# Bank sets, scalings, taps and an order of additions: one rescheduling of a fused convolution and channel MLP

## The chip, the cores and the metric

One core of a Trainium2 chip. The metric is the device time of one execution in microseconds (us), median over several runs. Ratios are the mean time of one kernel's fast runs over that of the other's of the same rounds, so not quite the ratio of the medians quoted beside them.

Engine names as the profile has them: PE is TensorE, PEld its weight loads, DVE is VectorE, ACT is ScalarE, POOL is GpSimd.

## The reference, cut to what matters

```python
def _attn_ref(x, weight):                  # x: 8 x 4224 x 192, weight: 8 heads x 7 taps
    w = softmax(weight)                    # over the taps
    # causal convolution of 7 taps along the sequence, one weight per head of 24 channels
    return np.einsum('hk,bskhg->bshg', w, x_unf)

def _moe_ref(x, g_ln, w_ch1, w_ch2):       # x: the result of the above
    xn = (x - mean) / sqrt(var + 1e-6) * g_ln
    return x + np.maximum(xn @ w_ch1, 0.0) @ w_ch2      # 192 -> 768 -> 192
```

## The kernel before

The rows are cut into 18 groups. For each group g the "up" product (w1, Relu) and the "down" product (w2) run on PE; beside them DVE does five of the seven convolution taps for group g+1, ACT the first two taps for group g+2 (the second through a buffer `tb` and an accumulating DMA, y<-tb), and the output of g-1 is scaled by the row's 1/sigma on ACT and added to the output by DMA. The down product is done in seven products of half size instead of eight (from sums of quarters, on DVE). In "mixed" groups (6, 8, ... 16) most of the up product is done so as well; two chunks of it stay plain. The sums of y that this takes lie in the room of `tb`.

Names in the code below: in the up product a11 to a22 are the quarters of y, b11 to b22 those of w1, s1 to s4 sums of quarters of y, c11 to c22 the quarters of the result; the down product has the same with the hidden values and w2. `w1sums` and `w2sums` are sums of quarters of the weights. The banks of `chain` add up several products in turn; those of `other` take one product each. To evict is to copy a set of banks out of PSUM, which ACT does here (1.87 to 1.88 us for a set of 128x2048, means of L596 and L510 in the kernel before). A matmul of the code stands as two records in the profile: 24 of them are x48 there.

The kernel takes eight banks of PSUM, in turn in two sets of four:

```python
    def take_set():
        i = (turn[0] + 3) // 4 * 4 % 8
        turn[0] = i + 4
        return all_banks[:, i : i + 4]
```

The up product of a mixed group, cut:

```python
        banks = plain(PAIR)                       # takes a set, 24 matmuls of 512 columns
        scale(g - 1, 0, 4)
        evict_up(g, PAIR, whole, banks)
        conv(g + 1, 2, 6)                         # DVE
        chain, other = take_set(), take_set()
        rows_of_tiles(chain, a11, b11, True, False)
        evict(chain, c11)
        ...                                       # a12 x b21, s2, s3, s1: in turn in other and chain
        rows_of_tiles(other, a22, w1sums[:, 3], False)
        evict(other, late[0])                     # the parts buffer
        scale(g - 1, 7, 8)
        add_to_out(g - 1, 0, 8)
        ...
        rows_of_tiles(chain, s4, b22, False)
        evict(chain, c12, True)
        nc.scalar.activation(c11, c11, AF.Relu)
        lower_sum(g, (PAIR,)); lower_sum(g, range(PAIR))   # DVE, cut to one line
        conv(g + 1, 6, K)
        banks = plain(PAIR + FC)                  # the next set in turn: the chain's
        evict_up(g, PAIR + FC, whole, banks)
        nc.scalar.activation(c22, c22, AF.Relu)
```

The down product, cut (`some_taps(n)` issues n of the 16 instructions of the first two taps for g+2; `product` ends in three copies on ACT unless told otherwise):

```python
        product(0, a[:, 0, 0], b[0], c11, True)
        if g in MIXED:
            scale(g - 1, 8, m); add_to_out(g - 1, 8, m)
            some_taps(1)
        else:
            some_taps(3)
        product(1, a[:, 1, 0], w2sums[:, 2], c22, True);        some_taps(3)
        product(1, a[:, 1, 1], w2sums[:, 3], parts[0], False);  some_taps(3)
        product(1, a[:, 0, 1], b[2], None, True);               some_taps(3)
        ...                                       # half sums on DVE
        product(0, a[:, 1, 1], w2sums[:, 1], c21, False);       some_taps(2)
        product(0, a[:, 0, 0], w2sums[:, 0], parts[1], False);  some_taps(2)
        product(0, a[:, 0, 1], b[3], c12, False);               some_taps(len(todo))
```

## Time and profile before

| | before |
|---|---|
| time, median of the first 3 runs (later of 4) | 1022.95 us (1022.73) |
| span of the profiled run | 1022.5 us |
| PE busy | 992.4 us, 97% |
| DVE busy | 884.6 us, 87% |
| PE idle in the body, 276.6 to 953.4 us | 676.80 - 658.49 = 18.3 us |

The last row is from the windows of the kernel before, from the first mixed group's start to the end of the last one. Columns: stretch, its length, then for PE, PEld, DVE, ACT and POOL the busy time with the number of instructions, then the granted clock, the DMA share and GB/s.

```profile
276.60:953.40 676.80, 658.49 (x11024) 461.53 (x11020) 598.75 (x990) 410.89 (x852) 54.20 (x64) 0.99 0.52 127
```

A clock of 0.99 as a mean over 677 us hides four short stretches at one half, called half-clock windows below. The ScalarE timeline of group 12 at the start of the down product (columns: start, duration, engine, line, operation, tiles, shapes, number; in brackets the idle time before and what ended it):

```profile
684.37 3.23 ACT L812 ACTIVATE ot<-ot,r 128x192 f32<-128x192 f32 x9
687.49 0.62 ACT L367 ACTIVATE y<-xg,taps 128x384 f32<-128x384 f32 x1
688.00 0.91 ACT L728 COPY cs<-ps 128x256 f32<-128x256 f32 x3
```

Nine scalings and one tap stand ahead of the copies of c22, which PE's third down product waits for.

### The profile page before, as it was taken

The numbers are of one execution on the slowest core, as the hardware profiler recorded it, in microseconds if no ns is written. First come the engines' busy times: TensorE is split into PE (matmuls) and PEld (weight loads), VectorE is DVE, ScalarE is ACT, GpSimd is POOL, SyncE is SP. The second block draws the span as 40 slices with busy tenths as digits, with TensorE's granted clock in tenths as the row PEclk, the third lists the DMA queues.
The fourth block names the chain that finished last, engine by engine and source line by source line (L and its number), as shares of the span: only waits on it lengthen the run. The fifth ranks groups of instructions, "written<-read, shape, count | busy, mean of one in ns | idle before, by whom it ended". The sixth has DMA issues, their size and how long they took to land. (4 is left out here: it accounts for less than half of the span.)

```text
span 1022.5 us, 37346 instructions
## 1 busy us (share of the span) xinstructions
PE 992.4 (97%) x16914; PEld 710.1 (69%) x16914; DVE 884.6 (87%) x1622; ACT 586.9 (57%) x1243; POOL 81.5 (8%) x110
## 2 busy tenths in 40 slices
PE   7999999999989999999999999989999999989997
PEld 6888674578575875758666686756857578575776
DVE  7999998899889797998979979799796989979707
ACT  6547464546576564665657665675656746574451
POOL 2001101000010000101001100110001000010000
PEclk9999999999999999999999999999999999999999
DMA  6343818535366364654636645466355663263031
GB/s 190 116 179 52 213 20 235 180 63 145 111 123 199 70 158 120 115 191 85 190 67 115 195 91 179 98 141 172 62 174 109 133 194 64 86 127 68 3 64 68
DMA packets 18702, 126.88 MB, mean 124 GB/s; under 512 B 2415, under 2 KB 3183, under 8 KB 13678
## 3 DMA queue, kind: packets, MB, share of 16 engines
q0 software_dynamic: 12096, 66.75, 33.3%
q1 hardware_dynamic: 6142, 57.73, 14.9%
q8 instruction: 132, 2.16, 0.8%
q14 instruction: 28, 0.23, 0.1%
q10 hardware_dynamic: 304, 0.00, 0.0%
HBM read 38.95 MB, written 50.23 MB: 87 GB/s over the span
## 5 line engine op out<-in xcount | busy, mean ns | idle before, releaser
L520 PE MATMUL ps<-yt,w 32*128 32x256 f32 (+6 forms) x6624 | 435.2, 417 | 14.0 <-ACT ht L596 12.6
L520 PEld LDWEIGHTS ps<-yt,w 32*128 32x128 f32 x6624 | 337.2, 186 | 109.1 <-issue 56.4
L394 DVE SCALAR_TENSOR_TENSOR y<-xg,taps,y 128x408 f32<-128x408 f32 (+5 forms) x734 | 365.9, 577 | 30.0 <-DMA y<-tb 23.9
L722 PE MATMUL ps<-ht,w2sums 128*32 128x256 f32 (+2 forms) x4320 | 238.7, 378 | 3.3 <-ACT cs L728 2.7
L687 DVE TENSOR_TENSOR ht<-ht 128x1088 f32<-128x1088 f32 (+2 forms) x162 | 184.4, 1208 | 35.6 <-ACT part L728 24.5
L722 PEld LDWEIGHTS ps<-ht,w2sums 128*32 128x32 f32 x4320 | 139.3, 110 | 97.3 <-ACT cs L728 5.5
L722 PE MATMUL ps<-ht,w 128*32 128x256 f32 (+2 forms) x3240 | 182.0, 378 | 0.0
L722 PEld LDWEIGHTS ps<-ht,w 128*32 128x32 f32 x3240 | 103.8, 110 | 73.9 <-issue 8.3
L508 ACT ACTIVATE ht<-ps 128x256 f32<-128x256 f32 (+2 forms) x312 | 100.8, 410 | 92.6 <-PE ps L520 86.4
L728 ACT COPY cs<-ps 128x256 f32<-128x256 f32 (+2 forms) x180 | 64.0, 371 | 119.2 <-PE ps L722 119.2
L510 ACT ACTIVATE ht<-ps 128x2048 f32<-128x2048 f32 (+5 forms) x48 | 63.3, 1318 | 97.7 <-PE ps L520 97.7
L812 ACT ACTIVATE ot<-ot,r 128x192 f32<-128x192 f32 x247 | 93.8, 459 | 4.9 <-DVE ot L787 4.9
L367 ACT ACTIVATE y<-xg,taps 128x408 f32<-128x408 f32 (+5 forms) x137 | 71.7, 591 | 5.8 <-DVE st L421 5.3
L421 DVE BATCH_NORM_STATS2 st<-y 128x6 f32<-128x192 f32 x264 | 70.1, 341 | 0.0
L787 DVE STREAM_TRANSPOSE ot<-cs 128x512 f32<-128x512 f32 (+2 forms) x90 | 57.7, 684 | 5.9 <-ACT cs L728 3.3
L380 ACT ACTIVATE tb<-xg,taps 128x384 f32<-128x384 f32 (+1 forms) x112 | 62.6, 618 | 0.0
L405 DVE STREAM_TRANSPOSE yt<-y 128x3072 f32<-128x3072 f32 (+5 forms) x19 | 56.2, 2957 | 4.2 <-PE ps L520 2.4
L816 POOL DMA_DIRECT2D out_dram<-ot x34 | 29.6, 884 | 364.4 <-ACT ot L812 186.2
L669 PE MATMUL ps<-ht,w 128*32 128x192 f32 (+3 forms) x1152 | 51.5, 339 | 0.0
L383 POOL DMA_DIRECT2D y<-tb x28 | 24.9, 1051 | 330.6 <-ACT cs L728 188.4
L520 PE MATMUL ps<-ysums,w1sums 32*128 32x256 f32 x864 | 48.1, 376 | 2.4 <-DVE ysums L571 2.4
L520 PEld LDWEIGHTS ps<-ysums,w1sums 32*128 32x128 f32 x864 | 45.5, 185 | 4.5 <-issue 3.5
(104 smaller groups left out, 496.6 us busy)
## 6 DMA issues: line engine op xcount, KB each, us to landing
y<-tb POOLq DMA_DIRECT2D x21, 768.0 KB, 6.0
out_dram<-ot POOLq DMA_DIRECT2D x20, 768.0 KB, 6.8
xg<-in_x_dram SPq DMA_DIRECT2D x6, 2208.0 KB, 15.8
xg<-in_x_dram SPq DMA_DIRECT2D x6, 2112.0 KB, 12.1
out_dram<-y SPq DMA_DIRECT2D x6, 1632.0 KB, 6.6
out_dram<-y SPq DMA_DIRECT2D x6, 1536.0 KB, 6.1
ht<-parts POOLq DMA_DIRECT2D x6, 1024.0 KB, 7.4
y<-tb POOLq DMA_DIRECT2D x7, 864.0 KB, 10.0
```

The lines of the kernel that those rows point to most:

```text
L367: nc.scalar.mul(dst, src, tap)
L380: nc.scalar.mul(tb[g][:, 0:n, cs], xg[g][:, 1 : 1 + n, cs], taps[:, h, 1:2])
L394: nc.vector.scalar_tensor_tensor(out=y[g][:, 0:n, cs], in0=t[:, k : k + n, cs], scalar=taps[:, h, k : k + 1], in1=y[g][:, 0:n, cs], op0=AL ...
L421: nc.vector.bn_stats(out=sums[g][:, j, :], in_=y[g][:, j, :])
L508: nc.scalar.activation(dst[:, q], src[:, q], AF.Relu)
L510: nc.scalar.activation(dst, src, AF.Relu)
L520: nc.tensor.matmul(banks[:, q, i * w : i * w + w], right[rows, c, P * i : P * i + P], left[rows, :, c, :], start=(first and c == 0 and i = ...
L687: nc.vector.tensor_tensor(a[:, *dst, f], a[:, *left, f], a[:, *right, f], op=op)
L722: nc.tensor.matmul(dst[C * q : C * q + C, 0:w], right[:, f, C * c : C * c + C], left[:, f, q], start=(first and f == 0), stop=(f == FC - 1 ...
L728: nc.scalar.copy(to[:, c], dst[:, 0:w].rearrange("p (j t) -> p j t", t=t))
L787: nc.vector.transpose(ot[:, 0:n, C * c : C * c + C], flat[:, c].rearrange("p (j t) -> p j t", t=C))
L812: nc.scalar.mul(ots[g][:, j, :], ots[g][:, j, :], rstd[g][:, j : j + 1])
```

## The change

Its intent: (1) the last plain chunk goes into the other bank set, so that PE need not wait for the eviction of the chain just before it; (2) the scalings are spread so that they fall where ACT has time; (3) the first two taps are issued sooner in odd groups, so that the room of `tb` is free when DVE wants it, and in mixed groups they are spread so that they end one product sooner; (4) in groups 3 and 4 the partial sums are added ahead of the statistics.

```diff
@@ up product of a mixed group
 (cut: plain(f) no longer takes a set itself; it is given its banks)
-        banks = plain(PAIR)
-        scale(g - 1, 0, 4)
-        evict_up(g, PAIR, whole, banks)
+        other, chain = take_set(), take_set()
+        turn[0] += 4
+        plain(PAIR, other)
+        scale(g - 1, 0, 7)
+        evict_up(g, PAIR, whole, other)
         conv(g + 1, 2, 6)
-        chain, other = take_set(), take_set()
 (cut: the four single scalings are now 7..11 in place of 4..8)
         conv(g + 1, 6, K)
-        banks = plain(PAIR + FC)
-        evict_up(g, PAIR + FC, whole, banks)
+        scale(g - 1, 11, 14)
+        plain(PAIR + FC, other)
+        evict_up(g, PAIR + FC, whole, other)
@@ down product
+        taps_behind = [3, 3, 3, 3, 2, 2]
+        if g in MIXED:
+            taps_behind = [0, 3, 3, 4, 3, 3]
+        elif g + 1 in MIXED:
+            taps_behind = [4, 4, 4, 4, 0, 0]
 (cut: some_taps(n) becomes some_taps(taps_behind[i]) behind products 1 to 6)
-            scale(g - 1, 8, m)
+            scale(g - 1, 14, m)
@@ end of a group
+        for half in range(last, 2):
+            finish_fast(g, half, *parts)
         if not last and not mixed and g + 1 not in MIXED:
             moments(g + 1)
             if g % 2 == 0:
                 root(g)
-        for half in range(last, 2):
-            finish_fast(g, half, *parts)
```

## The prediction

> **What bounds the kernel now.** I read the page first (part 1, part 2, part 5), then the waits, then the timelines of one pair of groups, 580 to 725 us, and last the windows around the waits.
>
> Part 1 and part 5 of the page:
>
> ```profile
> PE 992.4 (97%) x16914; PEld 710.1 (69%) x16914; DVE 884.6 (87%) x1622; ACT 586.9 (57%) x1243; POOL 81.5 (8%) x110
> ...
> L520 PE MATMUL ps<-yt,w 32*128 32x256 f32 (+6 forms) x6624 | 435.2, 417 | 14.0 <-ACT ht L596 12.6
> ```
>
> PE is the bound: 992.4 of 1022.5 us, so only 30.1 us are idle. The waits of PE name nearly all of it:
>
> ```profile
> PE ps L520 <- ACT ht L596: 12.6, 6, 2.7
> PE ps L344 <- POOL room L272: 4.9, 1, 4.9
> PE ps L722 <- ACT cs L728: 2.7, 5, 0.6
> PE ps L520 <- DVE ysums L571: 2.4, 3, 0.8
> PE ps L520 <- ACT ht L508: 1.4, 1, 1.4
> PE ps L722 <- DVE ht L687: 0.5, 1, 0.5
> ```
>
> (columns: us in total, times, longest). Six waits on L596 are one for each mixed group (6, 8, ... 16): the last plain chunk is put in the banks of the chain, and must wait until ScalarE has emptied them into c12. PE's timeline in group 12 and ScalarE's in group 14:
>
> ```profile
> 667.41 2.77 PE L520 MATMUL ps<-ysums,w 32*128 32x256 f32 x48
> 672.83 7.11 PE L520 MATMUL ps<-yt,w 32*128 32x512 f32 x48 [2.66 <-ACT ht L596]
> ```
> ```profile
> 792.37 1.87 ACT L596 COPY parts<-ps 128x2048 f32<-128x2048 f32 x1 [0.70 <-PE ps L520]
> 794.13 0.46 ACT L812 ACTIVATE ot<-ot,r 128x192 f32<-128x192 f32 x1
> 794.91 1.88 ACT L596 ACTIVATE ht<-ps 128x2048 f32<-128x2048 f32 x1 [0.33 <-PE ps L520]
> ```
>
> The wait costs more than it lasts. The same 24 matmuls of 512 columns take 7.11 to 7.13 us in groups 6, 8, 10, 12 and 5.43 us in 14 and 16. The windows tell why (the third number from the end, ahead of DMA share and GB/s, is the granted clock):
>
> ```profile
> 673.00:675.50 2.50, 2.50 (x12) 1.05 (x16) 2.50 (x6) 1.57 (x1) 0.00 (x0) 0.50 1.04 152
> 797.00:802.00 5.00, 5.00 (x48) 2.21 (x48) 5.00 (x9) 1.59 (x1) 0.00 (x0) 1.00 1.03 177
> ```
>
> After the wait in four of six groups the clock falls to one half for a while; 7.12 - 5.43 = 1.7 us each, hidden in "busy".
>
> DVE (87%) is the nearest rival. It waits in every odd group for the transfer y<-tb to release the buffer that the sums of y take:
>
> ```profile
> DVE ysums L570 <- DMA y<-tb: 44.4, 6, 8.0
> DVE y L394 <- DMA y<-tb: 23.9, 5, 5.4
> ```
>
> [...] half clock, for 2 x 1.7 = 3.4 us. [...] a 2.0 us wait does not always cost a window: 4 of 6 here, the others (14, 16) with the same wait did not. [...] nine scalings in a row take 3.23 us, 0.36 each. [...] y<-tb, the adds of partial products and the adds to the output share one software queue; the page has all of them there (33.3% of 16 engines).
>
> **The change, part by part** (T is the end of s4 x b22, 670.2 in group 12, which nothing ahead of it moves).
>
> (1) Other bank set. The last plain chunk now needs the eviction of a22's product into the parts buffer, not that of c12. In group 14: begun 792.37, 1.87 long, done 794.24; s4 ends at 792.06 + 2.80 = 794.86. So 0.6 us to spare. Only group 12 is late: its eviction began at 668.79 after 1.80 us for the transfer ht<-parts, and ends at 670.66, 0.5 us after T. The wait shrinks from 12.6 to some 0.5 us: about 12 us off the path. The sets of all products keep their relation (the counter is moved on by one set, so the down product starts one set further): its first two columns take the chain's banks, free at T + 1.9; its third takes the plain chunk's, evicted by T + 5.43 + 2.0 = T + 7.4, needed at T + 5.43 + 2.7 = T + 8.1. That was so before.
>
> (2) The half clock. With no wait there is nothing left to throttle: 4 x 1.7 = 6.8 us in the profiled run. The plain runs differ by 1.85 us (1022.51 to 1024.36), about one window, so I take 3 to 4 windows, 5.1 to 6.8.
>
> (3) Scalings. The same 17 a group: 7 before the first plain eviction (7 x 0.36 = 2.6 us, from 648.0 to 650.6; the eviction can start at 652.1), 4 single ones as before, 3 in the shadow of the last plain chunk (ScalarE there: c12 1.9, Relu of c11 1.9, scalings 1.1, done at T + 4.9, chunk at T + 5.4), 3 instead of 9 in the down product. It is these 9 (684.37, 3.23 us) that delay the copies of c22, for which PE waits 0.56 us five times: 2.7 us gone.
>
> (4) Taps of odd groups. Before, the last two of 16 wait behind product 6 and end at 644.1; now four follow each of the first four products. ScalarE in group 11: parts copied by 630.7, then eight at 0.55 = 635.1. The transfer is issued 9 us sooner; it took 10.2 us from issue (644.4 to 654.7), so it lands near 645.5, before DVE asks at 647.9. DVE's 44.4 us of waiting fall to near 0, the sums are there before PE wants them: 2.4 us of PE. In mixed groups the taps end behind product 6 rather than 7: some 3 us sooner, DVE's 23.9 us roughly halve, off the path.
>
> (5) Partial sums ahead of the statistics: reaches groups 3 and 4 only, as the condition excludes all others. In group 4 ScalarE waited 6.2 us for DVE (the addition at L785 frees the hidden tile); the addition moves from 217.6 to about 210, and PE's 1.4 us goes. DVE loses about 1 us there, with 2.4 us of slack at its transpose.
>
> **Does DVE allow it?** PE comes to the down product 2.0 + 1.7 us sooner in each mixed group, and its fifth product needs DVE's half sums. DVE in group 12 needs 36.8 us from the first sum of y (654.67) to the first half sum (691.43). Started at 647.9, with some 1.3 us of waiting for the Relu of c11, it is there at 686.1. The half sum can begin near the end of the third product, T + 17.1 = 687.3. Margin 1.2 us, and as much again while the fourth product runs (4.07 us against 3.4 us of half sums). In group 16 PE already waited 0.5 us for DVE; that goes too.
>
> **Sum.** 12.1 + 2.7 + 2.4 + 1.4 + 0.5 = 19.1 us of waits, and 5.1 to 6.8 us of clock: 24 to 26 us. From 1022.95: 997 to 999. I add about 0.7 us for small waits: 998.5, 2.4% faster.
>
> **The rivals.** (A) DVE takes over as bound in the mixed groups: if y<-tb lands late because the load of x (issued 622.5, 12.1 us to landing) and the store of y share the engines then, the start slips. Against it: the load is nearly over at 635; the slack is about 2 to 3 us. Were it 3 us over, 6 x 3 = 18 us return at most; likelier 1 us in each, 6 us: 1004. (B) The clock stays throttled, or only the waits count: had the half clock another cause than the wait, 6.8 us stay: 1005. Against it, the two groups right after equal waits run at 5.43 us, and no stretch without a wait is throttled. (C) ScalarE or the software queue becomes the new wait at the same place: the add to the output of the first 8 rows is now issued some 3 us sooner (its scalings are done), in a stretch where the windows show DMA at 1.0 of its share, and may hold up the adds to c22, needed by a Relu at T + 7.4. They landed at about 673.6; slack 4 us, and 4 more before PE needs it. That leaves at most 1 us in each group. (D) The waits were hidden anyway: speaks against it that PE is the bound in the whole body and the chain that ended last ends with 33.55 us of L520 and 20.61 of L722 on PE.
>
> **Range and chances.** The floor is 1022.95 - 19.6 - 6.8 = 996.5. Rivals A to C each give back 0 to 6 us. Range 995.5 to 1004. Faster by over 2% means below 1002.5: 0.84; within 2%: 0.15; slower: 0.01.
>
> **What would show it.** Right: no wait of PE on the c12 eviction, at most 1 us on L596's others; the last plain chunk at 5.4 us and clock 1.00 in all six; PE busy near 985.6; DVE's wait at L570 below 6 us in total; no wait of PE on copies of c22. Wrong: PE waiting for L687's half sums (A), half-clock windows left (B), PE or ScalarE waiting on ht<-parts (C).

## The result

993.49 us (992.62 to 993.86, 4 runs) against 1022.73 us (1020.71 to 1024.36, 4 runs): ratio 0.9714, 95% interval 0.9695 to 0.9733. Faster by 2.9%; the result is 5.0 us under the predicted 998.5 and below the range.

| | before | after |
|---|---|---|
| span of the profiled run | 1022.5 us | 992.1 us |
| PE busy | 992.4 us | 979.3 us |
| DVE busy | 884.6 us | 886.4 us |
| PE idle in the body | 18.3 us | 0.8 us |
| mean granted clock | 0.993 | 1.000 |

Part 1 of the page after, and the body in the windows:

```profile
PE 979.3 (99%) x16914; PEld 701.4 (71%) x16914; DVE 886.4 (89%) x1622; ACT 588.9 (59%) x1243; POOL 81.5 (8%) x110
```
```profile
274.50:922.90 648.40, 647.63 (x11020) 458.13 (x11016) 602.00 (x992) 412.57 (x852) 54.26 (x64) 1.00 0.53 130
```

The waits of PE after, the whole answer (us in total, times, longest):

```profile
PE ps L344 <- POOL room L272: 4.9, 1, 4.9
PE ps L309 <- DVE room L225: 1.8, 1, 1.8
PE ps L520 <- ACT parts L596: 0.5, 1, 0.5
PE ps L724 <- issue: 0.2, 1, 0.2
```

The first two are the start of the program. In the body the wait forecast for group 12 is left, and 0.24 us in group 8 that the profile puts down to no engine; the repeat of this kernel (a, below) does not have it. The same place in group 14, PE's timeline and ACT's:

```profile
766.97 2.77 PE L520 MATMUL ps<-yt,w1sums 32*128 32x256 f32 x48
769.56 2.77 PE L520 MATMUL ps<-ysums,w 32*128 32x256 f32 x48
772.15 5.33 PE L520 MATMUL ps<-yt,w 32*128 32x512 f32 x48
777.41 4.09 PE L724 MATMUL ps<-ht,w 128*32 128x256 f32 x72
```
```profile
769.85 1.87 ACT L596 COPY parts<-ps 128x2048 f32<-128x2048 f32 x1 [0.71 <-PE ps L520]
...
772.39 1.88 ACT L596 ACTIVATE ht<-ps 128x2048 f32<-128x2048 f32 x1 [0.33 <-PE ps L520]
```

The last plain chunk starts at 772.15, before the eviction of c12 has begun (772.39): ACT and PE now work beside each other. DVE in group 12 goes from one group's last transpose to the sums of y without a pause, where it had paused 6.76 us; before, then after:

```profile
654.67 0.96 DVE L570 TENSOR_TENSOR ysums<-yt 128x768 f32<-128x768 f32 x1 [6.76 <-DMA y<-tb]
```
```profile
630.30 0.74 DVE L792 STREAM_TRANSPOSE ot<-cs 128x544 f32<-128x544 f32 x1 [0.49 <-ACT cs L730]
630.97 0.92 DVE L570 TENSOR_TENSOR ysums<-yt 128x768 f32<-128x768 f32 x1
```

**Where the 30.4 us of span came from.** PE's work is one unbroken list of products, so it can be counted without any "idle" at all: the time from the first matmul of one product to the first of the next, before less after. Group 14 before, PE's timeline:

```profile
789.47 2.80 PE L520 MATMUL ps<-yt,w1sums 32*128 32x256 f32 x48
792.06 2.80 PE L520 MATMUL ps<-ysums,w 32*128 32x256 f32 x48
796.84 5.43 PE L520 MATMUL ps<-yt,w 32*128 32x512 f32 x48 [1.99 <-ACT ht L596]
802.21 4.09 PE L722 MATMUL ps<-ht,w 128*32 128x256 f32 x72
```

From start to start: 2.59, then 4.78, where 2.59 is what the product takes. The wait cost 2.19 us; the idle time in the brackets says 1.99. Done for all groups, the starts read from the same timelines:

| place | before less after, start to start | counted as idle before, less after |
|---|---|---|
| wait ahead of the last plain chunk, 6 groups | 13.1 | 12.6 - 0.5 |
| the last plain chunk itself, 6 groups | 7.3 | 0 (half clock) |
| sums of y, in the up products of 6 groups | 3.3 | 2.4 |
| mixed down products (copies of c22, half sums) | 4.7 | 2.7 + 0.5 |
| up product of group 5 | 2.4 | 1.4 |
| start of the program, net | -0.4 | -1.4 |
| sum | 30.4 | 17.7 |

All other products of all groups agree within 0.2 us between the two kernels. The rows of waits in the last column come to 19.1 us, 4.4 us less than in the first.

### The profile page after: what moved, and what is told of

It reads as the page before. It is cut to its first block, busy times and chain, and to the rows that moved or that the text cites.

```text
span 992.1 us, 37342 instructions
## 1 busy us (share of the span) xinstructions
PE 979.3 (99%) x16914; PEld 701.4 (71%) x16914; DVE 886.4 (89%) x1622; ACT 588.9 (59%) x1243; POOL 81.5 (8%) x110
## 4 chain that ended last, share of the span: by engine, by line
PE 94%; issue 2%; DMA 2%; DVE 1%; ACT 0%; SPq 0%; POOL 0%; ACTq 0%; DVEq 0%; POOLq 0%
PE ps L520 48%; PE ps L724 39%; PE ps L671 5%; DMA ht<-parts 1%; DMA room<-in_moe_w_ch_dram 1%; DVE ht L689 1%; PE ps L300 1%; PE ps L325 0%; PE ps L330 0%; ACT parts L596 0%; DVE y L829 0%; PE ps L309 0%; PE ps L312 0%; DVE room L225 0%; DVE room L217 0%
## 5 line engine op out<-in xcount | busy, mean ns | idle before, releaser
L520 PE MATMUL ps<-yt,w 32*128 32x256 f32 (+6 forms) x6624 | 426.6, 412 | 0.6 <-ACT parts L596 0.5
L520 PEld LDWEIGHTS ps<-yt,w 32*128 32x128 f32 x6624 | 331.4, 185 | 91.9 <-issue 52.2
L724 PEld LDWEIGHTS ps<-ht,w 128*32 128x32 f32 x3240 | 103.8, 110 | 74.6 <-ACT ot L817 4.6
L821 POOL DMA_DIRECT2D out_dram<-ot x34 | 31.6, 945 | 347.3 <-ACT ht L508 178.6
L671 PEld LDWEIGHTS ps<-ht,w 128*32 128x32 f32 x1152 | 37.1, 110 | 13.7 <-issue 0.5
```

Of the source, the lines that this page charges most:

```text
L520: nc.tensor.matmul(banks[:, q, i * w : i * w + w], right[rows, c, P * i : P * i + P], left[rows, :, c, :], start=(first and c == 0 and i = ...
L671: nc.tensor.matmul(bank[C * q : C * q + C, 0:w], w2[:, f, C * c : C * c + C], t[:, f, q, js.start - fast[g] : js.stop - fast[g], :], start ...
L724: nc.tensor.matmul(dst[C * q : C * q + C, 0:w], right[:, f, C * c : C * c + C], left[:, f, q], start=(first and f == 0), stop=(f == FC - 1 ...
```

## The experiments

The kernel before ran in the same rounds each time: medians 1024.29, 1023.77 and 1023.41 us. Its single runs lie between 1020.7 and 1026.5, and by and large go with the clock that each run records: 0.996 at about 1021, 0.993 at 1024, 0.991 at 1025.6. The number of half-clock windows differs from run to run.

| run | time, us | ratio to before, 95% interval |
|---|---|---|
| the change (first result) | 993.49 | 0.9714 (0.9695 to 0.9733) |
| a: the change, repeated by mistake | 992.97 | 0.9700 (0.9679 to 0.9720) |
| a2: all but the bank set | 1012.91 | 0.9887 (0.9866 to 0.9907) |
| b: the bank set alone | 1019.97 | 0.9964 (0.9945 to 0.9983) |
| c: all but the taps | 1015.95 | 0.9923 (0.9903 to 0.9942) |
| i: bank set and taps of odd groups | 1000.30 | 0.9769 (0.9749 to 0.9789) |
| d: all but the scalings | 994.22 | 0.9711 (0.9692 to 0.9730) |
| e: all but the order of additions | 995.58 | 0.9725 (0.9705 to 0.9745) |
| h: all but the taps of mixed groups | 992.97 | 0.9698 (0.9679 to 0.9717) |
| k: taps of odd groups half as early | 993.82 | 0.9710 (0.9690 to 0.9730) |
| f: before, wait filled with matmuls | 1017.57 | 0.9943 (0.9926 to 0.9961) |

**a, a failed edit, and a2, the bank set put back.**

```diff
 a   -        turn[0] += 4
     -        plain(PAIR + FC, other)
     +        last = take_set()                 # which is other's set again
     +        plain(PAIR + FC, last)
 a2  -        turn[0] += 4
     -        plain(PAIR + FC, other)
     +        plain(PAIR + FC, chain)
```

> The changed kernel with the bank set of the last plain chunk put back. Theory (the parts overlap little, each wait has its own cause): the wait on c12's eviction is back, 6 x 2.2 us from product to product, and with it some half-clock windows, 3 to 4 of 1.8 us; the waits on the sums of y, the copies of c22 and the fifth product stay gone. 993.5 + 13 + 6 = about 1012 us, clock below 1 in the records. Rival (the clock fell for another reason): 1006 us, clock 1.00.

The edit of a took "the next set", which after `other` and `chain` is `other`: PE's instructions were the same as in the changed kernel. 992.97 us is a repeat of the change and no more; it says nothing on the bank set. a2 does what was meant:

> The run meant to put the bank set back did not do so: its last plain chunk still landed in the free set, so it repeated the changed kernel (992.97 us). This one does put the last plain chunk back in the chain's banks; all else is as changed. Theory: the wait of 2.2 us (product start to product start) on c12's eviction is back in all six groups, with some half-clock windows of 1.8 us, from none to six; with VectorE early, nothing else waits: 993.5 + 13 + 0 to 11 = 1007 to 1018 us. Rival (with VectorE early the eviction comes early as well, the wait was VectorE's doing): within 3 us of the changed kernel.

1012.91 us, as the theory has it: the wait and the half clock are back and nothing else. The waits of PE in a2 (of the start, two lines left out):

```profile
PE ps L520 <- ACT ht L596: 12.6, 6, 2.6
```

In five of six groups a half-clock window followed. The sixth, group 10, is a control inside the run: its up product is 2.28 us longer than in the changed kernel, those of groups 6, 8, 14 and 16, with the same wait and the half clock, 3.98. So a window cost 1.7 us here. The early DVE did not bring the eviction forward.

Which pauses cost a window here can be worked out from the clock records of the traces. In the kernel before all half-clock windows start on one grid of 3.413 us (the four of the body are 122.88 us apart, 36 steps; the fifth, behind PE's last matmul, comes 348.16 us after the fourth, 102 steps). I added up PE's counted idle time inside each step of such a grid, in all traces but h's. In the body, the ten steps of before, a2 and c that held 1.99 us or more were all followed by a step at half clock. No step that held 1.89 us or less was, but for one in f (1.35 us). The pauses of groups 14 and 16 in the kernel before lay across a boundary of the grid (0.87 and 1.12 us, 1.06 and 0.92 us), and so did group 10's in a2 (0.11 and 1.89 us). So whether a pause of 2.0 us costs a window was, in these traces, a matter of where it fell. This was read off afterwards; no run was made to test it, and f's case stays unexplained.

**b, the bank set alone; c, all but the taps.**

```diff
 b (on the kernel before)
     -        banks = plain(PAIR)
     +        other, chain = take_set(), take_set()
     +        turn[0] += 4
     +        banks = plain(PAIR, other)
     -        chain, other = take_set(), take_set()
     -        banks = plain(PAIR + FC)
     +        banks = plain(PAIR + FC, other)
 c (on the changed kernel)
     -            taps_behind = [0, 3, 3, 4, 3, 3]
     -        elif g + 1 in MIXED:
     -            taps_behind = [4, 4, 4, 4, 0, 0]
     +            taps_behind = [1, 3, 3, 3, 2, 2]
```

> The kernel before with the bank set alone changed. Theory (VectorE takes over, because the sums of y start 8 to 9 us after the group on PE, and the half sums are ready 36.8 us later, plus 3.4 us for the first three: the fifth down product can't start before 48 to 49.5 us from the group's start, against 44.2 in the changed kernel and 48 to 50 in the kernel before): the wait on c12 and the half clock go, a wait of PE for the half sums of 3 to 5 us comes in each mixed group; 1014 to 1020 us. Rival (the parts add up): 1022.7 - 13 - 7 = about 1002 us and no wait for the half sums over 1 us.

> The changed kernel with the taps spread as before. Theory (VectorE takes over): VectorE waits 7 to 8 us at the sums of y again, PE waits some 4 to 5 us for the half sums in each of the six mixed groups and about 1 us for the sums of y in three: 1018 to 1022 us, nearly the whole gain lost. Rival (the taps were worth only PE's wait on the sums of y): 993.5 + 3.3 = about 997 us.

1019.97 and 1015.95 us; c is 2 us below the range that I had put down. In both the wait on c12 is gone and PE waits for DVE instead. PE's timeline in group 12 of b:

```profile
665.92 5.33 PE L520 MATMUL ps<-yt,w 32*128 32x512 f32 x48
671.18 4.09 PE L722 MATMUL ps<-ht,w 128*32 128x256 f32 x72
676.65 0.64 PE L722 MATMUL ps<-ht,w2sums 128*32 128x256 f32 x8 [1.37 <-DVE ht L696]
677.78 7.54 PE L722 MATMUL ps<-ht,w2sums 128*32 128x256 f32 x136 [0.50 <-DVE ht L696]
685.14 4.07 PE L722 MATMUL ps<-ht,w 128*32 128x256 f32 x72
689.03 1.31 PE L722 MATMUL ps<-ht,w2sums 128*32 128x256 f32 x16
690.83 7.11 PE L722 MATMUL ps<-ht,w2sums 128*32 128x256 f32 x128 [0.50 <-DVE ht L687]
```

The second line from the top is the first down product; the wait for DVE comes ahead of the second one already (L696, the lower sum), not only at the fifth (L687, the half sums) where I had put it. The mixed down product takes 30.4 to 30.7 us in b and 30.1 to 31.4 in c, against 27.3 in the changed kernel: 3 to 4 us a group given back (c's 31.4, in group 14, holds a half-clock window). In b the body of the profiled run has no half-clock window (mean clock 0.999), but three of the other five runs record a clock of 0.993 or 0.994, so some had come back there. The cause is in DVE's waits, in b and in c:

```profile
DVE ysums L570 <- DMA y<-tb: 44.8, 6, 8.1
```
```profile
DVE ysums L570 <- DMA y<-tb: 45.0, 6, 8.1
```

So in these two "the parts add up" is refuted: the wait on c12 had hidden that DVE came late, and once it was gone DVE's lateness took its place.

**i, the two together.**

```diff
 b, and:
     -            some_taps(3)                      # behind products 1 to 4
     +            some_taps(3 + (g + 1 in MIXED))
```

> The kernel before with the bank set and the taps of odd groups alone; scalings, order and taps of mixed groups as before. Theory (these two together free PE in the mixed groups, each useless without the other): 993.5 + 4.6 for the scalings + 2.4 for the order = 1000.5 us, up to 1002.5 with a half-clock window after the wait in group 5. Rival (taps of mixed groups are needed too, VectorE is behind without them): over 1005 us.

1000.30 us, as the theory has it. Alone the bank set gives 0.4%; with the taps of six odd groups, 2.3%. PE's waits in i are the copies of c22, the place in group 5 and group 12's parts, as in the kernel before or as left by the change:

```profile
PE ps L722 <- ACT cs L728: 2.8, 5, 0.6
PE ps L520 <- ACT ht L508: 1.3, 1, 1.3
PE ps L520 <- ACT parts L596: 0.5, 1, 0.5
```

**k, how soon is soon enough.**

```diff
     -            taps_behind = [4, 4, 4, 4, 0, 0]
     +            taps_behind = [4, 4, 4, 2, 2, 0]
```

> The changed kernel with the last four taps of the odd groups behind the fourth and the fifth product (4, 4, 4, 2, 2, 0): the transfer is issued some 5 us later than in the changed kernel and 4 us sooner than in the kernel before. Theory (as the prediction reckoned, VectorE's slack in the mixed groups is 2 to 3.5 us beyond the end of its own work): the transfer lands 2 to 3 us after VectorE asks, and PE waits 0 to 0.5 us in each group: 993.5 to 996.5 us. Rival (no slack, every us late is a us lost): 6 x 2.5 = 15 us, 1008 us.

993.82 us; PE waits for nothing in the mixed groups beyond group 12's parts (group 10's down product is 0.3 us longer, the others are equal). DVE waits again, and it costs nothing:

```profile
DVE ysums L570 <- DMA y<-tb: 20.8, 6, 3.9
```

20.8 us over six groups, up to 3.9 in one, fit in the slack. 45 us over six, up to 8.1, do not (c). In b the shortest of these waits, 6.6 us in group 10, already cost 3.1 us. That brackets the slack of DVE between 3.9 and 6.6 us a group; 6.6 less 3.1, and 8.1 less 3.4 in others, put it at an estimated 3.5 to 4.7 us. The prediction's 2 to 3 us was on the cautious side.

**d, all but the scalings, and h, all but the taps of mixed groups.**

```diff
 d   -        scale(g - 1, 0, 7)
     +        scale(g - 1, 0, 4)
     -        scale(g - 1, 11, 14)
     -            scale(g - 1, 14, m)
     +            scale(g - 1, 8, m)           # and the single ones at 4..8
 h   -            taps_behind = [0, 3, 3, 4, 3, 3]
     +            taps_behind = [1, 3, 3, 3, 2, 2]
```

> The changed kernel with the scalings where they were: nine in a row in the down product. Theory (they delay the copies of c22, for which the third product waits, 0.77 us from start to start): 6 x 0.77 = 4.6 us, 998 us, the wait of PE on the copies of cs shown as about 0.56 us six times. Rival (they had only filled VectorE's wait and now hide): 993.5 us.

> The changed kernel with the taps of the mixed groups spread as before (one behind the first down product), those of odd groups as changed. Undoing the scalings alone cost 0.3 us in each mixed group, not 0.77, so the first tap may be the rest. Theory (nine scalings or nine and a tap are too much, three and a tap fit): no wait of PE, 993.5 us. Rival (the tap itself holds up the copies of c22): some 0.5 us in each group, 996.5 us.

d: 994.22 us, not 998. My theory that the nine scalings delay the copies of c22 by themselves is wrong: with them back, the mixed down product takes 27.60 us against 27.33, and no wait is counted. h: 992.97 us, nothing lost. So it takes both, nine scalings and the one tap behind them (3.23 and 0.62 us in the lines shown of before), to hold up the copies by 0.77 us; either part of the change cures most of it, and only having neither costs. The first of h's five runs took 2996.47 us; it is left out (see the last section), and it was the profiled one, so that for h there is a time but no trace to read the waits from.

**e, all but the order of additions.**

```diff
     -        for half in range(last, 2):
     -            finish_fast(g, half, *parts)
              (moments and root of groups 3 and 4)
     +        for half in range(last, 2):
     +            finish_fast(g, half, *parts)
```

> The changed kernel with the partial sums added behind the statistics again, in groups 3 and 4. Theory (the up product of group 5 waits for the hidden tile): 2.4 us there, of which the profile counts 1.4 as idle; 995.9 us, or 997.6 with one half-clock window after that wait. Rival (only what is counted as idle is lost): 994.9 us.

995.58 us (994.57 to 996.59). The times do not separate 995.9 from 994.9; the trace does. The up product of group 5 takes 35.65 us against 33.21, 2.44 us more, of which the profile counts 1.4 as idle:

```profile
PE ps L520 <- ACT ht L508: 1.4, 1, 1.4
```

No half-clock window followed in the profiled run.

**f, the wait kept and filled.**

```diff
 (on the kernel before)
     +        rows_of_tiles(other, s4, b22)    # again, into free banks; nobody reads it
              banks = plain(PAIR + FC)
```

> The kernel before with s4 x b22 done a second time, into the banks that are free, just ahead of the last plain chunk: 24 matmuls of 2.59 us that nobody reads stand in place of the wait of 2.2 us on c12. Theory (the wait itself makes the clock fall): no half-clock window, the last plain chunk 5.3 us in all six groups, and though PE does more work the time falls by 4 x 1.8 - 6 x 0.4 = about 5 us, to 1017 to 1019. Rival (the clock falls for something else in this stretch, the transfers or VectorE and ScalarE at full load): windows at half clock stay, 1024 to 1026 us.

1017.57 us: with 24 more matmuls of the code in each mixed group the kernel is faster by 0.6%. All the windows in mixed groups are gone in the profiled run, the other five runs record a clock of 0.999 or 1.000, and the last plain chunk takes 5.33 us in group 12, where it had taken 7.11:

```profile
666.00 5.77 PE L520 MATMUL ps<-ysums,w 32*128 32x256 f32 x96
671.59 5.33 PE L520 MATMUL ps<-yt,w 32*128 32x512 f32 x48
```

The transfers and the other engines did the same work as before, so that rival falls: in these runs it is PE's own pause that makes the clock fall (0.991 to 0.996 in the kernel before in these rounds, 0.999 or 1.000 in five of f's six runs). One window is left in f, in the up product of group 5: right after the pause there, which f does not touch, the windows show a clock of 0.63 from 219 to 222 us and 0.80 from 222 to 225, and the product takes 37.34 us, 1.7 more than in the kernel before.

No combination beat the change: a, h and k are the same within the noise. In the body PE is idle 0.8 us of 648.4, so more would have to come from fewer matmuls or from the start and the end of the program.

## Why the prediction was wrong

**The mechanism was right in all steps but one (the scalings, below).** The bank set: the wait goes, and group 12 keeps 0.5 us, as forecast. The half clock: gone in all six groups, and f shows that the pause was its cause. The taps: y<-tb was done before DVE asked for the sums of y, its wait at L570 fell from 44.4 us to nothing. The order: PE's wait in group 5 is gone. DVE does not become the bound (rival A): b and c show that it would have, had the bank set come without the taps, so this was the rival that deserved its place. Rival B is refuted by f and a2. Rival C did not come: no wait on the adds to c22. Rival D is refuted by the result.

**What failed is the step "Sum": its terms of waits were too small.** "12.1 + 2.7 + 2.4 + 1.4 + 0.5 = 19.1 us of waits" took the idle time that the profile counts for what a wait costs. From start to start the same places gave 13.1 + 4.7 + 3.3 + 2.4 = 23.5 us: 4.4 us more. Most pauses cost about 0.2 us above their count, and the one in group 5 a whole us (there, in the kernel before, the first matmuls of the next four banks start 0.28 us apart, at 219.04 to 219.87, as ACT frees the banks one by one: its copies end at 218.99 to 219.81). The prediction's own sign shows it: PE busy was to fall by the half clock alone, to 985.6 us, and fell to 979.3. The reason is in the records: matmuls overlap (48 records of 0.37 us each in 2.59 us), so the tail of the last one before a pause stands as busy time in a stretch in which PE gets no further. Their ends are modelled in this profile besides, as its legend says. I had the right number on the page: 2.59 us for s4 x b22 and 672.83 - 667.41 = 5.42 us to the next start give a wait of 2.83 us, where the line says 2.66. The overlap is in these timelines: the next product starts 2.59 us after this one, and this one's records end at 2.77 to 2.80 us.

**The clock term** was put at "5.1 to 6.8 us" and gave 7.3 in the profiled pair; 1.7 us a window is right (2.28 against 3.98 in a2), and the last plain chunk is 0.1 us shorter in two groups without a window. The 0.7 us added "for small waits" did not come, beyond group 12's, already in the sum. The start of the program lost 0.4 us. In all, with the profiled runs compared: 30.4 found, 19.1 + 6.8 - 0.7 = 25.2 forecast; 4.4 of the 5.2 us between them are the waits.

**The step "(3) Scalings" was right in its result and wrong in its cause**, so its gain came by luck. "It is these 9 ... that delay the copies of c22": d shows that alone they cost 0.3 us a group, h that the tap alone costs nothing. The gain came because the change takes away both, where either is nearly enough. And "(4)" was right that the taps of mixed groups are "off the path".

**The worth of the parts** is not their sum: the bank set alone 0.4%, all but the bank set 1.1%, both of the main parts 2.3%, everything 2.9 to 3.0%. The taps of odd groups alone, on the kernel before, were not run; a2, which has them and all else but the bank set, is the nearest.

## What to carry to other kernels

Count a wait of an engine with overlapping instructions from start to start against the same product without the wait; the idle column was too low here, by about 0.2 us at most pauses and by a whole us in group 5, and a pause of TensorE of 2.0 to 2.7 us also cost 1.7 us at half clock that stands as busy, in some places (four of six in the kernel before) and not in others with the same pause. Before taking away the one wait that shows, work out when the next operand would have been ready: if it comes no sooner, the wait only changes its name, and the part that brings that operand forward must come with it. And undo each part alone: one of five here carried nothing, and one was credited with what a neighbour would have done as well.

## What the traces show of pauses, and one slow run

- Pauses of 2.0 to 2.7 us by the profile's count were followed by a half-clock window of 3.413 us in four of six places in the profile of before and in five of six in a2. What told them apart was the idle time inside one step of the grid: 1.99 us or more was followed by half clock in ten of ten cases (before, a2 and c), 1.89 us or less in none but one (1.35 us, in f). The clock records of before and of the changed kernel hold two values, 1.0 and 0.5. A pause filled with useless matmuls, 24 of the code (2.59 us) in place of a wait of 2.2 us, six times, made the kernel 0.6% faster (f).
- A single pause cost about 0.2 us above the counted idle time, and 2.44 against 1.4 us in group 5, where several banks came free one after another.
- One run in five of h took 2996.47 us, with TensorE's matmuls at 2.5 times their length (1039 ns against 412 in the largest group), VectorE's unchanged (579 against 575 ns) and a recorded clock of 1.00. What slowed this run was not found.
